# Regrouping the head loads of a one-core attention and gMLP block, taking an early weight load out of the head, and making the instruction order anew

## Chip, cores, metric

The kernel runs on one core of one Trainium2 chip. The metric is the device time in microseconds (us). All times compared below come from runs that were classed as fast, unless the text says otherwise. The sets of runs were made on different chips of the same kind, so each time is to be read against the "before" of its own rounds.

## The reference

The input x has 2048 tokens of 512 values, in bf16.

```python
def _A_ref(x, wqkv, wo):            # called on layernorm(x)
    qkv = split_heads(x @ wqkv)     # 32 heads of 16
    q, k, v = qkv[0], qkv[1], qkv[2]
    phi = lambda t: jnp.where(t > 0, t + 1, jnp.exp(t)) + 1e-06
    pq, pk = phi(q), phi(k)
    kv = einsum('bhsd,bhse->bhde', pk, v)
    ...                             # linear attention, then @ wo
h  = x + _A_ref(layernorm(x), A_wqkv, A_wo)
h2 = h + _B_ref(layernorm(h), B_w_in, B_w_sp, B_b_sp, B_w_out)   # gMLP; w_sp mixes tokens
```

## The kernel before

x is worked on in 16 tiles of 128 tokens, called x0 to x15. The head of the program does this for each tile: load, layernorm statistics and aggregate on VectorE, reciprocal standard deviation `rs` (ScalarE or GpSimd), normalised tile `xn` (VectorE for tiles 0 to 5, ScalarE after that), transposed tile `xnT` (TensorE and a ScalarE copy for tiles 0 to 5, a DMA transpose after that), the "K matmuls" of xnT and wk on TensorE, and then exp, minimum and `pk` on ScalarE and VectorE.

Nothing here is ordered at run time. A Python layer records every operation with its data dependencies and then replays a stored order. That order gives each engine its instruction stream. Waits are generated from the dependencies.

```python
    def schedule(self):
        ids = np.frombuffer(zlib.decompress(base64.b85decode(ORDER)), np.uint16).tolist()
        ...
        self.order = {e: [o for o in self.seq if o.eng == e] for e in self.ENGS}
...
    # loads of the head; first_load puts them behind each other on a queue,
    # `behind` makes the queue wait until another load has landed
    x0 = load_x("SP", 0, 1, 2150)
    load_x("ACT", 1, 1, 2250)
    x2 = load_x("SP", 2, 1, 2500)
    load_x("ACT", 3, 1, 2500)
    wk = [first_load(eng, wqkv[:, c:c + 2, D:2 * D], A_wqkv[c * P:(c + 2) * P, D:2 * D], f"wk{c}", 3500)
          for eng, c in (("SP", 0), ("ACT", 2))]
    for n, lat, behind in ((4, 2000, x2), (6, 2200, x2), (8, 1900, wk[0]), (10, 2100, wk[0]), ...):
        load_x("SP", n, 2, lat, behind)
...
    def stats(src, k, n):
        s = st[k][:, n, :]
        dve(lambda v: v.bn_stats(s[:, 0:6], src[:, n, :]), [src[:, n, :]], [s[:, 0:6]], D)
        return dve(lambda v: v.bn_aggr(s[:, 6:8], s[:, 0:6]), [s[:, 0:6]], [s[:, 6:8]], 14)
...
    warmup(34, 103)                               # matmuls on zeros, no result used
...
        # in k_unit(n), for the two tiles n, n + 1:
                op = stats(x, 0, i)
                if i == 0:
                    second = warmup(16, 60, op)   # waits for the aggregate of x0
...
    # spatial weights, 16 blocks of 128 rows; the first EARLY of them go into the head as whole loads
    for i, t in enumerate(order):
        w = NT // 2 if EARLY <= i < NT // 2 else NT
        for j in range(0, NT, w):
            op = dma_t(wsp[:, j:j + w, t * P:(t + 1) * P], B_w_sp[...], f"wsp{t // TPG}", ...)
```

## Time and profile before

| | before |
|---|---|
| median of the first three runs | 234.14 us |
| span of the profiled run | 231.8 us |
| TensorE (PE) busy | 97% |
| first transposes / first K matmul | 6.35 / 7.90 us |
| K matmuls of tiles 6 and 7 begin | 18.58 us |

The profile page of before gives the span, then busy time with its share of the span and the instruction count for each engine. Further down it gives the shares of the chain of work that ended last.

```profile
span 231.8 us, 3231 instructions
...
PE 224.6 (97%) x1180; PEld 112.1 (48%) x1203; DVE 161.6 (70%) x323; ACT 104.3 (45%) x193; POOL 44.2 (19%) x134
...
PE 86%; DMA 6%; ACT 3%; DVE 2%; issue 1%; SPq 0%
```

TensorE bounds the kernel. The parts of the chain that are not PE lie mostly in the head, and the timeline of PE shows where. Its columns are start, duration, engine, line, operation, operands and count, and in brackets the idle time before it and what ended that.

```profile
1.04 5.51 PE L594 MATMUL psum<-warm 128*128 128x128 bf16 x50 [1.04 <-POOL warm L439]
6.35 1.43 PE L570 MATMUL psum<-ident,xn 128*128 128x128 bf16 x16
7.90 3.52 PE L402 MATMUL psum<-wqkv,xnT 128*128 128x512 bf16 x15
...
14.63 2.75 PE L655 MATMUL psum<-pk,xn 128*128 128x512 bf16 x12
18.58 1.90 PE L402 MATMUL psum<-wqkv,xnT 128*128 128x512 bf16 x7 [1.20 <-DMA xnT<-xn]
```

After the first microsecond one idle stretch stands out, 1.20 us before the K matmuls of tiles 6 and 7. They waited for a DMA transpose. The sync queue's timeline shows what that transpose had to stand behind:

```profile
8.86 5.56 SPq L435 DMA_TRANSPOSE wsp<-in_B_w_sp_dram  x1
14.47 6.10 SPq L435 DMA_TRANSPOSE xnT<-xn  x4
```

The early spatial-weight load holds the queue from 8.86 to 14.42 us. The VectorE timeline of before, from its start:

```profile
3.36 0.70 DVE L511 BATCH_NORM_STATS2 st<-x 128x6 f32<-128x512 bf16 x1 [3.36 <-DMA x<-in_A_x_dram]
4.09 0.18 DVE L512 BATCH_NORM_AGGREGATE st<-st 128x2 f32<-128x6 f32 x1
4.19 1.25 DVE L511 BATCH_NORM_STATS2 st<-x 128x6 f32<-128x512 bf16 x2
5.36 0.30 DVE L512 BATCH_NORM_AGGREGATE st<-st 128x2 f32<-128x6 f32 x2
5.58 0.38 DVE L556 TENSOR_SCALAR xn<-x,st,rs 128x512 bf16<-128x512 bf16 x1
```

The statistics of x0 are aggregated 0.73 us after they began, x2 and x3 follow, and xn0 begins at 5.58 us.

### The profile page before, as it was taken

The numbers are of one execution on the slowest core, as the hardware profiler recorded it, in microseconds if no ns is written. First come the engines' busy times: TensorE is split into PE (matmuls) and PEld (weight loads), VectorE is DVE, ScalarE is ACT, GpSimd is POOL, SyncE is SP. The second block draws the span as 40 slices with busy tenths as digits, with TensorE's granted clock in tenths as the row PEclk, the third lists the DMA queues.
The fourth block names the chain that finished last, engine by engine and source line by source line (L and its number), as shares of the span: only waits on it lengthen the run. The fifth ranks groups of instructions, "written<-read, shape, count | busy, mean of one in ns | idle before, by whom it ended". The sixth has DMA issues, their size and how long they took to land.

```text
span 231.8 us, 3231 instructions
## 1 busy us (share of the span) xinstructions
PE 224.6 (97%) x1180; PEld 112.1 (48%) x1203; DVE 161.6 (70%) x323; ACT 104.3 (45%) x193; POOL 44.2 (19%) x134
## 2 busy tenths in 40 slices
PE   8997999999999999999999999999999999999995
PEld 8543444453445443454544444444455555555452
DVE  4998755646987550237489989979795566785485
ACT  5694754399989876679862010101021211123010
POOL 3436300000466608023771000000000000000000
PEclk9999999999999999999999999999999999999999
DMA  5893259947546635968999700000000000020025
GB/s 182 263 214 70 59 138 230 315 147 181 114 89 136 117 71 121 183 126 188 185 228 197 159 3 0 0 0 0 3 0 1 0 3 0 20 72 3 0 80 191
DMA packets 58864, 23.68 MB, mean 102 GB/s; under 512 B 48480, under 2 KB 58720, under 8 KB 58848
## 3 DMA queue, kind: packets, MB, share of 16 engines
q1 hardware_dynamic: 58144, 22.88, 44.7%
q10 hardware_dynamic: 704, 0.59, 0.8%
q8 instruction: 9, 0.15, 0.3%
q14 instruction: 7, 0.06, 0.1%
HBM read 7.47 MB, written 2.10 MB: 41 GB/s over the span
## 4 chain that ended last, share of the span: by engine, by line
PE 86%; DMA 6%; ACT 3%; DVE 2%; issue 1%; SPq 0%
PE psum L402 70%; PE psum L802 6%; PE psum L655 5%; PE psum L805 4%; DMA x<-in_A_x_dram 3%; DMA xnT<-xn 2%; DMA hnT<-hn 1%; DVE st L511 1%; ACT sh L421 1%; ACT xn L421 1%; ACT e L421 0%; ACT xnT L421 0%; PE psum L751 0%; PE psum L676 0%; PE psum L720 0%
## 5 line engine op out<-in xcount | busy, mean ns | idle before, releaser
L421 ACT ACTIVATE psum<-psum 128x256 f32<-128x256 f32 (+1 forms) x33 | 14.3, 445 | 90.8 <-PE psum L402 63.1
L402 PE MATMUL psum<-wsp,z 128*128 128x512 bf16 x204 | 47.5, 379 | 0.2
L402 PEld LDWEIGHTS psum<-wsp,z 128*128 128x128 bf16 x208 | 20.4, 98 | 22.9
L402 PE MATMUL psum<-hnT,win 128*128 128x512 bf16 x108 | 25.6, 379 | 0.2
L421 ACT ACTIVATE e<-psum 128x1024 bf16<-128x1024 f32 (+1 forms) x18 | 16.7, 926 | 15.2 <-PE psum L402 14.3
L402 PE MATMUL psum<-t,s 128*128 128x512 bf16 x94 | 22.1, 379 | 0.1
L421 ACT ACTIVATE z1T<-psum 128x512 bf16<-128x512 f32 x28 | 16.6, 594 | 4.9 <-PE psum L402 4.8
L802 PE MATMUL psum<-win,hnT 128*128 128x512 bf16 x64 | 16.4, 379 | 0.4 <-DMA hnT<-hn 0.4
L402 PE MATMUL psum<-wout,z1T 128*128 128x256 bf16 (+1 forms) x82 | 16.6, 314 | 0.1
L402 PEld LDWEIGHTS psum<-hnT,win 128*128 128x128 bf16 x112 | 10.0, 98 | 13.2 <-ACT z1T L421 3.8
L402 PE MATMUL psum<-wqkv,xnT 128*128 128x512 bf16 x61 | 14.8, 380 | 1.4 <-DMA xnT<-xn 1.2
L421 ACT ACTIVATE z<-psum 128x896 bf16<-128x896 f32 x16 | 14.5, 909 | 2.9 <-PE psum L805 2.8
L402 PE MATMUL psum<-xnT,wqkv 128*128 128x512 bf16 x61 | 15.1, 379 | 0.3 <-issue 0.2
L655 PE MATMUL psum<-pk,xn 128*128 128x512 bf16 x64 | 15.3, 379 | 0.0
L402 PE MATMUL psum<-m,pqT 128*128 128x512 bf16 x62 | 14.7, 379 | 0.3 <-DVE h L776 0.2
L776 DVE SCALAR_TENSOR_TENSOR h<-psum,x 128x512 bf16<-128x512 f32 x16 | 10.8, 688 | 5.2 <-PE psum L402 5.1
L402 PEld LDWEIGHTS psum<-t,s 128*128 128x128 bf16 x96 | 9.4, 98 | 10.3
L582 DVE TENSOR_SCALAR e<-e 128x1024 bf16<-128x1024 bf16 (+1 forms) x18 | 7.1, 397 | 9.1 <-ACT e L421 9.0
L805 PE MATMUL psum<-win,hnT 128*128 128x384 bf16 x64 | 13.0, 326 | 0.0
L924 DVE TENSOR_TENSOR u<-psum,bsp 128x512 bf16<-128x512 f32 x16 | 11.0, 687 | 2.8 <-PE psum L402 2.7
L556 DVE TENSOR_SCALAR z<-z,st,rs 128x896 bf16<-128x896 bf16 x16 | 7.2, 493 | 7.3 <-POOL rs L519 7.3
L511 DVE BATCH_NORM_STATS2 st<-x 128x6 f32<-128x512 bf16 x15 | 9.7, 677 | 3.6 <-DMA x<-in_A_x_dram 3.6
(113 smaller groups left out, 349.3 us busy)
## 6 DMA issues: line engine op xcount, KB each, us to landing
r<-rcp SPq DMA_DIRECT2D x16, 128.0 KB, 2.6
out_dram<-h SPq DMA_DIRECT2D x15, 128.0 KB, 1.8
win<-in_B_w_in_dram SPq DMA_DIRECT2D x2, 896.0 KB, 6.6
x<-in_A_x_dram SPq DMA_DIRECT2D x6, 256.0 KB, 4.5
wqkv<-in_A_wqkv_dram SPq DMA_DIRECT2D x2, 512.0 KB, 5.2
wout<-in_B_w_out_dram SPq DMA_DIRECT2D x1, 896.0 KB, 7.2
wo<-in_A_wo_dram SPq DMA_DIRECT2D x1, 512.0 KB, 8.3
bsp<-in_B_b_sp_dram SPq DMA_DIRECT2D x1, 512.0 KB, 5.1
```

The lines of the kernel that those rows point to most:

```text
L402: inst = pe.matmul(out_ap, lhsT=a, rhs=b, start=start and i == 0, stop=stop and i == len(pairs) - 1, **kw)
L421: return g.add("ACT", lambda ac: ac.activation(out_ap, in_ap, func, **kw), [in_ap, *extra], [out_ap] + ([accum] if accum is not None else []),
L511: dve(lambda v: v.bn_stats(s[:, 0:6], src[:, n, :]), [src[:, n, :]], [s[:, 0:6]], D)
L556: return dve(lambda v: v.tensor_scalar(dst, src, mean, rst, op0=ALU.subtract, op1=ALU.mult), [src, mean, rst], [dst], w + 460, acc=4)
L582: dve(lambda v: v.tensor_scalar(e, e, 1.0, EPS_PHI, op0=ALU.min, op1=ALU.add), [e], [e], w * GW, acc=4)
L655: inst = pe.matmul(bank(CB[c]), lhsT=xn[:, i, c * P:(c + 1) * P], rhs=pk[:, i, :], start=i == 0, stop=i == NT - 1)
L776: dve(lambda v, n=n, b=b, s=s: v.scalar_tensor_tensor(h[:, n, :], bank(b), 1.0, x[:, n, :], op0=ALU.mult, op1=ALU.add, accum_out=s[:, 0:1] ...
L802: pe.matmul(bank(b), lhsT=hnT[:, c, n * P:(n + 1) * P], rhs=win2[:, c, 0:GW], start=c == 0, stop=c == KD - 1)
L805: inst = pe.matmul(bank(b + 1, F2), lhsT=hnT[:, c, n * P:(n + 1) * P], rhs=win2[:, c, GW:FH], start=c == 0, stop=c == KD - 1)
L924: dve(lambda v: v.tensor_tensor(t, bank(b), add, ALU.add), [bank(b), add], [t], GW, ps=True)
```

## The change

Its intent is to issue fewer and larger loads in the head and to free the sync queue from the early spatial-weight load. The stored order was made anew for this, so the streams of all engines differ. The diff, cut (the two ORDER strings are left out, some switches that are off, and a number of the load of wq). The numbers in the thousands are the times to landing, in ns, that the schedule's model assumes:

```diff
-EARLY = 1
+EARLY = 0
-ORDER = "c-jTQ17HvU..."
+ORDER = "c-jrpgMttU..."
-    x0 = load_x("SP", 0, 1, 2150)
-    load_x("ACT", 1, 1, 2250)
-    x2 = load_x("SP", 2, 1, 2500)
-    load_x("ACT", 3, 1, 2500)
-    wk = [first_load(eng, wqkv[:, c:c + 2, D:2 * D], A_wqkv[c * P:(c + 2) * P, D:2 * D], f"wk{c}", 3500)
-          for eng, c in (("SP", 0), ("ACT", 2))]
-    for n, lat, behind in ((4, 2000, x2), (6, 2200, x2), (8, 1900, wk[0]), ...
+    load_x("SP", 0, 1, 2250)
+    load_x("ACT", 1, 1, 2350)
+    x2 = load_x("SP", 2, 2, 3250)
+    wk = first_load("ACT", wqkv[:, :, D:2 * D], A_wqkv[:, D:2 * D], "wk", 3900)
+    for n, lat, behind in ((4, 1500, x2), (6, 1700, x2), (8, 2000, wk), ...
```

What the new order does to the start of VectorE's stream can be read from the built programs without running them:

```
before: stats x0 | aggr x0 | stats x2, x3 | aggr x2, x3 | xn0 | xn2, xn3 | xn1 | stats x4, x5 ...
after:  stats x0 | stats x4 | aggr x0, x4 | stats x2, x3 | xn0 | aggr x2, x3 | xn1 | stats x5 | xn2, xn3 ...
```

More of the change, by code (lines that the diff above doesn't have):

```diff
@@ L13 @@
 GRAN = 16
-EARLY = 1
+EARLY = 0
 SEM_NS = 45.0
-ORDER = "c-jTQ17HvU00h8Cwq47%ZQHhO+qGrewr$(CZ5wwH5gAbt9Wf9Su@D<^5Eu2800D@ED2Rr5$b~$}jl4*LqyUHz2nE3iiC_qhWJrz_NQp#9j8w>n{3w9JNQ(-ngvO|hifD@XNQl%(gMui6bjW~0NROh(gp4SL;;4eE$c!dvhAgOttSEtOsEO>Tj&A6I?kI_#D23)|fpBPrmgt4v=!-tcfm*16wy2FdXpPdSi+UJ`GAN7sXn-*oi}6^7B{+=bSc-PYiE=294rqh+XoyA_fPol{e&~-u=!i}@g3dUILzsYxn1sn#foYh6Ay|pf2#+ubi&cn#)i{b{IDz9BieU)ENCaUNMq>@uVLGOw3%X(^W?%v4<1|iU78YVH*5eGG;uKz@fg0)sp5qy2V-AL61U6tJ7GW`VU^_NpGqzwZ=3x)^VkdTCH_qWK_F+E`U@Nxa3a;WjF5n_A;U+HQ8gAh_Zr~N(;5FXjHtypN?&2OEA~+u)1Vi#2BJdF+G7{h8F`nQjKHvvF;uk*QAHLu-zTqprBPPMH49!ps!&o$9Gb*DoGNUja<1-H9G91J6H)1dqQ!@`UGdlA!3-hx8(=aX5F+DRdBQvoaOS2ZqeEfr~EJ*P$$}kwSF*|cGCkwGWb1{GkSeQjvl*L$=3Au#z*pj)~gSA<lCE13Fn3xr~m}Oa?OIe4l*qXiBmVH=}l~|co*p6$smJQgDjaZfK*^@Qcm`&J=eVLTWS%RgQgvq#t$(4dlnUc-9hbgp-TbWvEG@MgdjoUbaBiWA~*pZ#sp99#L138Gxxt%+>f-5<d={22=)L1pSjx(4+d%2HY*p1EDg4LN)sgzl1704hC<zRMaR}SM4Hc=L(Q$~$qCQai^o?%vHQ+DN0PUTiE<y9W#S3VU`K^0aZ713E9VR02z2^CXml~fs(S1Fa%9UkQ|-sKg(;Z>H?6TW2y&EkF@;6bkE25#hNj^S92<4*44A&%#4&f#3H;yg~^ah~9OF63cO;wEn9J>KU7KIBQB;yb?Q2cF}3Uf@OU=4r0xHD2c>HdQk<R|~aND^2DCPUIq1RAp7tA3o(X{$&+a)fawcHHBAeB~u%<RXep;2X#~@bygR3RRn!waD`A!g;Xtl<a6HOO+MlazT_>w;wS!NL|x`<J|+}NRAhbU5B}sY-e!CyP!xqyXh~rdRbgcXD4~8ckrFG3s;h>gD~3KZreZ0!!YP`PDvshRnBr-G`e?9ftFC6Kj%I3zhN_+hs;_2ixVmYIrfQJ7tG{|^l~!w-rYle*HCMybQzO(*qclz%G+MnBr16@ddFrkC8lzd7sC8PPC0eMpO5(Aaqyw6xrCOuOTBh~dsLfiWE!wJs+NPvltP@(U?b@Xk+N71*p}jh+L)xvK+Nb?GqCGmQ<4Wk0I;GP(qeMQY#LnfjI;RvquM4`QD@y5$itl8;rcb)A54x<Yx}&?grJK5^+`g{|O6>#=@JBt;L#6U#J<|(4(Nm@MXT8=drE_{e*B8CiS7q=!z125;*AFFk7XQ*uW%O_T6a7bjmEXZ^!*XbcabAaX2#0lehjSWda#m+{HWzR~M{q<(avn!@WJh-t7jkw-a|{=DKF4t^$8-+obP*SIF_&>!7k3HQbA88kBR6&vH*hmIbxD_ULr-!GH+OlrbSw9A8~1h}w{}IBb|qK#1o!hq_jP{{a67kkdk^#=5AiTp@nBbVIoEInS95jObS>9*M|bu{*Ku8UcMnhTR8MmUZ}Mgj^(+r}Cy(?DPxlsg@np|*kViPsvpvsqJl6}n$V)um3%%G&J<g-u)nmQfqrA+kywYpD*6SSG!F@yV+|!}F)$jF2x7E#KyxJ=~-s`==+q~U7ywkh<AMVe{ZU"
@@ new lines @@
+ORDER = "c-jrpgMttU00qE@tj)G<d$VoZwz=81ZQHhO+jiZ}H%vrCMr;Hi5~3g~q9HnBASPlVF3KVv${`1GArTS-AdFxLh2RK>5D>y60+JvpLLwQGBLNa31#%)cQlmWbAP(XqB~l?T@}VFqpaB{o4bmYk@*@!GkpTrz7=@4-4UrLzQ4y6;8JUm;U6B=?(G6Wt4MoueP0<|9&>cO{3!%{pMNkFVkR8=g6)jK$B~TN!&=;dH8pTi?B~c2sF$Q%o7Io1YEzu99Q3h?%2K7)M1F!^3u?UNC5IxZweb66aFb?A}5zDX~6VMJ*FbOL$5NpsL9k3q<FbIb*7{f3WD{vS`a1>!N9IJ2)Couve(Gi_66_YU?(=ZQnF$2djA2TrvYq1(9a0<^+M^Et#k5N}o5QHIEk9Amph1iCz*no}LgxQ#bUD%E7*n=I|iPJcPz1WA%*n-QrgtIt@^SFTPxQHvbfvdQN7kG(Rc#WI5i#xcDTeuJN9)dAA-yj?xAUq@R8{Xm}9^oB6;5**qBR(M-zu+(a;0HeAD}Es~LoozHGCE^0fRP!A5gC?05r)5!f+?Ac8JU++8HJgcig6f|u^Ef0nTBbZj`>)E>6x2kX8!xXOG)Nu9%f-yW@C01U_l155DT+9OH<6jGK|Z3ti|}uz?@vfW~|MwEW#Qr#^x-=1Wd@Xtiy#|%$DrIRjkPtT+KvG%%UvE@~ps$ti;Of#-3clx~#|gY`}&r&P`0J%}l0U+``>V!lZ1(CQQcUoWzu>r}}EjDs087Y|X7~!(I$xcMfAUHfAdI<~B~|9uDVT4q<YoRSJz@IxS@%wq-lEXJ7VX2d36k4rLnkXJ>ZgH16X7uHhhNR3@cYR%K9TWm8UN(G*T+b{%3a<xpPb)?wyT9-U%-on`^e;7o4kNbct-&f;wD;AoEF9FAotcHv+SWI+{DpbD#qZn3CJsHASQm@cunj&L03axLfc3@7j`&v7Tu^8zn&9glJu*Rz2ds*&dLGOzF|ukjeKb2*Q5JR7TtnrZ<jvYE=Ll*+2KUhy^G@DA_t9`Exl-|-QD@iCjLg<7hWTC0uPDv8>uy*j9)I;pd6@I5#11W)n-SMVWMvYg86H~;W2H}W4pv63q2GoSDaD=VzRsiHpcDZ}e4zwrPM@+Q9%qMq?1BPc+U6->cZP1W^-KN(TaSw&S9M{yNJQ58?|l|Ui%f*}=2p%hxtlu*$XLot;|Vf2!bl~}P9Tm95aE7e>5RYSEjNYgb~Gc-iA)J0v@O#?JsBQ#mV6r_QgqNy6Gu^OsznxopPslMv29_pj<nydL*ubCR9dFrXr8l%~ornQ=&#hR$Z-mi69pbeU&RobLATB3zoq@~)d)mo;l+NJ~As4d#5<yxWb+M^xXt9?4GT{^DhKA{9Ysna^8BRZ=yI;Rxgt@k>rLpr8|O5&V8uZy~@RKBLGO6Ci?q$|3uJG!YGx~mVmuY^wIdy4CadZ3hkq^EkW$9kePj^~&9q*sdXw0@=+`m8TX?_5sjH+rkD`lxUEuFU?aANr+y{;j`)^Z1WaJE?8?pXg8y?JN%N5Dw#T4(kjK?+DKA07rI2M|DPLb$(}aCTDj6M|UJgaWv;}UKezr3pti!yNC<BsEav<i@SvDxsFS@w0pRL8@i{<x{({ZiJQ8Y>$;Ddxwredulu{X>${{YxT4E@fLnNwgWSpk-O_E`+HGCNm0a1?JkjMm-c>xolU&s`UEMWY%e6h&?YzO0J;hVK(L+7l9lXiyJ;XCT&C@-@!#u(rJ<D@F+jBhM3%%I$yugdR#3S9=quj}3Jl5U3)Lp&8E4|E{z1nNM*6SR{!5q@J^iHo8)1!S|T|Ca+y~<m>-0Qv7+q~U7ywm>y1b4@<"
@@ L487, in load_x @@
         return first_load(eng, x[:, n:n + w, :], x_d[n * P:(n + w) * P, :], f"x{n}", lat, behind)
-    x0 = load_x("SP", 0, 1, 2150)
-    load_x("ACT", 1, 1, 2250)
-    x2 = load_x("SP", 2, 1, 2500)
-    load_x("ACT", 3, 1, 2500)
-    wk = [first_load(eng, wqkv[:, c:c + 2, D:2 * D], A_wqkv[c * P:(c + 2) * P, D:2 * D], f"wk{c}", 3500)
-          for eng, c in (("SP", 0), ("ACT", 2))]
-    for n, lat, behind in ((4, 2000, x2), (6, 2200, x2), (8, 1900, wk[0]), (10, 2100, wk[0]), (12, 2300, wk[0]),
-                           (14, 2500, wk[0])):
+    load_x("SP", 0, 1, 2250)
+    load_x("ACT", 1, 1, 2350)
+    x2 = load_x("SP", 2, 2, 3250)
+    wk = first_load("ACT", wqkv[:, :, D:2 * D], A_wqkv[:, D:2 * D], "wk", 3900)
+    for n, lat, behind in ((4, 1500, x2), (6, 1700, x2), (8, 2000, wk), (10, 2200, wk), (12, 2400, wk), (14, 2600, wk)):
         load_x("SP", n, 2, lat, behind)
-    first_load("SP", wqkv[:, :, 0:D], A_wqkv[:, 0:D], "wq", 3400)
+    first_load("SP", wqkv[:, :, 0:D], A_wqkv[:, 0:D], "wq", 3500)
     exp_table = g.add("ACT", lambda ac: ac.preload_act_table_set("natural_log_exp_and_others"), [], [], cost=1300)
@@ L611, in bass_sequential_preLN__linear_attn_block__mixer_gmlp__prompt_kernel @@
     HEAD, SINGLE = 6, 4
-    ACTS = (1,)
+    ACTS, ND, LEAD, lead = (1,), (), 0, []
     QSPLIT, KSPLIT, CACT = (6, 7), (), 2
@@ L618, in k_unit @@
         b = next_pair()
+        first = len(g.ops)
         for i in (n, n + 1):
@@ L631, in k_unit @@
                     rstd_act(st[0], rs[0], i, 1, 6)
+        if n == 2 and LEAD:
+            for op in g.ops[first:]:
+                if op.eng == "DVE":
+                    op.soft.add(lead[LEAD - 1].i)
         if n == 2:
@@ L634, in k_unit @@
         elif n:
-            rstd(st[0], rs[0], n, 2, 6, n >= HEAD)
+            rstd(st[0], rs[0], n, 2, 6, n >= HEAD or n in ND or n + 1 in ND)
         for i in (n, n + 1):
-            norm("DVE" if n < HEAD else "ACT", xn[:, i, :], x[:, i, :], st[0], rs[0], i, 6, D)
+            lead.append(norm("DVE" if n < HEAD and i not in ND else "ACT", xn[:, i, :], x[:, i, :], st[0], rs[0], i, 6, D))
             if n < HEAD:
@@ L647, in k_unit @@
             for i in (n, n + 1):
-                phi(pk[:, i:i + 1, :], b + i % 2, 1)
+                phi(pk[:, i:i + 1, :], b + i % 2, 1, i in KSPLIT)
         else:
```

## The prediction

> **What bounds the kernel now.** From about 18.6 us to the end TensorE does. The busy table gives PE 224.6 of 231.8 us, and the chain that ended last is PE for 86% of the span, almost without a gap after 18.58 us. So only the head can win or lose time. There the chain runs: x0 and x2 landed (to 4.00), the load of x4/x5 that was queued behind x2 (4.00 to 7.58), VectorE statistics and xn (to 11.48), ScalarE, then two DMA transposes (14.47 to 18.58). The waits view has one PE wait of note, 1.2 us for xnT at 17.4 us; the timeline of the sync queue shows why: the spatial-weight transpose occupies it from 8.86 to 14.42. VectorE is 99% busy from 10 to 20 us.
>
> **What the change does.**
> 1. Removes that 5.56 us issue. Worth at most the 1.2 us PE wait (0.5%). The same bytes come later as two half loads, well before the spatial matmuls at 118.8 us[...]: about 0.
> 2. x2 and x3 as one 256 KB load on the sync queue, wk as one 512 KB load on the scalar queue: the same 1 MB, two issues fewer (about 0.45 us each). x0, x1 as before (3.4 us). But "x2" now lands only when 256 KB have moved, with wk beside it: about 4.8 us instead of 3.98, estimated from the bytes per slice of before. The loads of x4 and x6 wait for x2, so x4 lands at about 7.7 us (7.2 to 8.5).
> 3. The reordering is the important part. In the new VectorE stream the second statistics instruction is that of x4, ahead of the aggregate of x0. [...] So x0's aggregate, which ran at 4.09 us, waits for x4's landing: about 8.4. Then two more statistics (1.25 us) precede xn0: about 10.0 instead of 5.58. xn2 and xn3 come 4 to 5 us later than before.
>
> **On the critical path.** Stepping through the new orders with durations of the trace (statistics 0.6, xn 0.35, copy 0.5, exp 0.6, pk 0.6, four K matmuls 0.87): first transposes at 10.0 instead of 6.35, first K matmul at 11.3 instead of 7.90, pk0 to pk3 about 4 us later, K matmuls of tiles 6 and 7 at about 21.4 instead of 18.58. The 1.2 us saved is inside this. PE has no later gaps in which to regain the rest: +2.8 us.
>
> PE also has nothing to do from about 4.8 to 8.4 us, since the second warm-up group waits for x0's aggregate. [...] In before the 50 warm-up matmuls took 5.5 us (about 110 ns each), while K matmuls started 0.22 us apart. I allow 0.7 us for cold matmuls.
>
> **Prediction:** 237.6 us (80%: 235.4 to 239.6). Faster by over 2%: 1%; within 2%: 74%; slower by over 2%: 25%.
>
> **Right if** the VectorE timeline shows one statistics instruction at 3.4 us, a gap of about 4 us ended by the load of x, and xn0 near 10 us; PE idle before the second warm-up group; the first K matmul at 11 to 12.5 us; a constant shift of 2.5 to 4.5 us from 25 us on.
>
> **Wrong if** x4 lands near 6.5 us (then +1.5), if matmuls run cold to 16 us or later (+1.5 more), or if wv and wo, now behind other late loads, land after their need at 50 to 55 us (a new wait, up to 2 us). If VectorE did not block on x4, the result would be about 232.8.

## The result

| | before | after |
|---|---|---|
| median, fast runs of the same rounds | 233.76 us (232.53 to 234.48) | 236.41 us (235.51 to 237.18) |
| ratio after / before | | 1.0117, 95% interval 1.008 to 1.0153 |
| first transposes / first K matmul | 6.35 / 7.90 us | 10.19 / 11.51 us |
| K matmuls of tiles 6 and 7 begin | 18.58 us | 22.45 us |

A ratio is the mean time of one kernel's fast runs over that of the other's fast runs of the same rounds, so it is not quite the ratio of the medians. A second set of five rounds of the same kernel is the yardstick for three later experiments.

**after_again.** Edit: none.

> The kernel after, unchanged, timed again in five rounds as the yardstick for the next three: ratio to before 1.009 to 1.014.

Measured: 236.19 us against 233.22, ratio 1.0131 (1.0104 to 1.0159). The change makes the kernel about 3 us slower, within the 2% band but clear of noise.

From here on the kernel after has line numbers of its own: L508 and L509 are its statistics and aggregate, L553 its xn, L591 its warm-up, L567 its transposes. Its page:

```profile
span 235.2 us, 3244 instructions
...
PE 227.0 (97%) x1203; PEld 113.0 (48%) x1203; DVE 161.3 (69%) x323; ACT 104.0 (44%) x193; POOL 44.2 (19%) x134
...
PE 90%; DMA 4%; DVE 2%; ACT 1%; SPq 1%; issue 0%
```

The busy shares are those of before, so they do not tell what happened. The VectorE timeline does:

```profile
3.55 0.69 DVE L508 BATCH_NORM_STATS2 st<-x 128x6 f32<-128x512 bf16 x1 [3.55 <-DMA x<-in_A_x_dram]
7.68 0.69 DVE L508 BATCH_NORM_STATS2 st<-x 128x6 f32<-128x512 bf16 x1 [3.43 <-DMA x<-in_A_x_dram]
8.29 0.30 DVE L509 BATCH_NORM_AGGREGATE st<-st 128x2 f32<-128x6 f32 x2
8.50 1.25 DVE L508 BATCH_NORM_STATS2 st<-x 128x6 f32<-128x512 bf16 x2
9.67 0.40 DVE L553 TENSOR_SCALAR xn<-x,st,rs 128x512 bf16<-128x512 bf16 x1
```

The second line is the statistics of x4. VectorE stood idle for 3.43 us until x4 landed. The data for the next useful instruction, the aggregate of x0, had been there since about 4.2 us. xn0 begins at 9.67 instead of 5.58 us. The PE timeline of after:

```profile
1.04 3.54 PE L591 MATMUL psum<-warm 128*128 128x128 bf16 x34 [1.04 <-POOL warm L439]
8.51 1.89 PE L591 MATMUL psum<-warm 128*128 128x128 bf16 x16 [3.92 <-DVE st L509]
10.19 1.06 PE L567 MATMUL psum<-ident,xn 128*128 128x128 bf16 x8
11.51 1.89 PE L402 MATMUL psum<-wqkv,xnT 128*128 128x512 bf16 x4 [0.26 <-ACT xnT L421]
13.19 1.06 PE L567 MATMUL psum<-ident,xn 128*128 128x128 bf16 x8
...
22.45 1.89 PE L402 MATMUL psum<-wqkv,xnT 128*128 128x512 bf16 x8
```

PE was idle for 3.92 us ahead of the second warm-up group. The first four K matmuls took from 11.51 to 13.19 us, 0.42 us each, where before needed 0.22. The granted clock explains that. The next view gives, for PE, the busy time in each stretch, its clock, and the DMA share and rate:

```profile
6.00:8.00 2.00, 0.00 (x0) 0.89 0.86 271
8.00:10.00 2.00, 1.49 (x15) 0.50 0.96 299
10.00:12.00 2.00, 1.74 (x14) 0.50 1.03 345
12.00:14.00 2.00, 2.00 (x12) 0.50 0.37 131
14.00:16.00 2.00, 2.00 (x12) 0.90 0.00 0
```

The clock was at half rate from about 7.6 to 14.4 us: a mean of 0.89 over 2 us means 2 x (1 - 0.89) / 0.5 = 0.44 us at half rate before 8.00, and likewise 0.4 us after 14.00. Tiles 6 and 7 begin 3.87 us later than before. After 22 us nothing adds to this. A little is given back: before had waits of 0.3 us (for ScalarE's m) and 0.4 us (for a DMA transpose of hn) between 55 and 66 us which after does not have, and the first spatial matmul block stands at 123.67 us against 120.32, 3.35 us later. The spans differ by 3.4 us.

These are the traces of the costlier kind of run of after. Of its 12 timed runs in the two sets, the four with a mean clock of 0.985 or 0.986 took 236.88 to 237.50 us, and the other eight 235.50 to 236.56 us. Both profiled runs are among the four. So the 3.4 us of the traces lie above the 2.65 and 2.97 us of the medians.

Why would an order put the statistics of x4 second? The kernel's own file suggests an answer. The time model in its `schedule` was replayed. In after the model starts the load of x4 at 1.00 us and has its data at 3.00 us, counted from the first load, which the trace has at 0.79 us. The trace has 4.85 and 7.65 us. The load of x4 must wait until x2 has landed. But in after x2 is also the load just ahead of it on its queue, and the model counts no landing time for an operation that is listed as such a neighbour. In before the half wk stood between them, and the model started x4 at 3.54 us. That the new order was made with this model is likely, but not shown.

### The profile page after: what moved, and what is told of

Read it like the earlier page. It is cut to its first block, busy times and chain, and to the rows that moved or that the text cites. A ratio compares the mean times of both kernels' runs of the same rounds, so it can differ in the third digit from the quotient of the medians.

```text
span 235.2 us, 3244 instructions
## 1 busy us (share of the span) xinstructions
PE 227.0 (97%) x1203; PEld 113.0 (48%) x1203; DVE 161.3 (69%) x323; ACT 104.0 (44%) x193; POOL 44.2 (19%) x134
## 4 chain that ended last, share of the span: by engine, by line
PE 90%; DMA 4%; DVE 2%; ACT 1%; SPq 1%; issue 0%
PE psum L402 72%; PE psum L657 6%; PE psum L804 6%; PE psum L807 4%; DMA x<-in_A_x_dram 3%; DMA r<-rcp 1%; PE psum L591 1%; SPq L744 1%; PE psum L567 1%; DVE h L778 1%; DVE pqT L766 1%; ACT pqT L421 0%; PE psum L678 0%; PE psum L687 0%; PE psum L753 0%; ACT r L421 0%
## 5 line engine op out<-in xcount | busy, mean ns | idle before, releaser
L402 PE MATMUL psum<-hnT,win 128*128 128x512 bf16 x112 | 26.1, 379 | 0.0
L402 PE MATMUL psum<-wqkv,xnT 128*128 128x512 bf16 x64 | 16.2, 397 | 0.3 <-ACT xnT L421 0.3
L508 DVE BATCH_NORM_STATS2 st<-x 128x6 f32<-128x512 bf16 x15 | 10.0, 678 | 7.0 <-DMA x<-in_A_x_dram 7.0
L553 DVE TENSOR_SCALAR hn<-h,st,rs 128x512 bf16<-128x512 bf16 x16 | 6.2, 406 | 11.3 <-POOL rs L544 11.0
L820 DVE BATCH_NORM_STATS2 st<-z 128x6 f32<-128x512 bf16 x9 | 6.1, 690 | 9.7 <-ACT z L421 9.7
```

Source lines behind the costliest of these rows:

```text
L402: inst = pe.matmul(out_ap, lhsT=a, rhs=b, start=start and i == 0, stop=stop and i == len(pairs) - 1, **kw)
L553: return dve(lambda v: v.tensor_scalar(dst, src, mean, rst, op0=ALU.subtract, op1=ALU.mult), [src, mean, rst], [dst], w + 460, acc=4)
L820: dve(lambda v, n=n, s=s: v.bn_stats(s[:, 0:6], z2[:, n, 0:GW]), [z2[:, n, 0:GW]], [s[:, 0:6]], GW)
```

## The experiments

Two theories stood against each other. The *order theory* says that the loss is VectorE's wait for x4 ahead of the aggregate of x0. The *load theory* says that the loss comes from x2, x3 and wk landing later. A third question is how much of the loss is the cold clock, that is, matmuls at half rate (the first four K matmuls of after took 0.42 us each, where before needed 0.22). All times are medians, and "before" is that of the same rounds. The programs were built again: each differs from its parent in the instructions named and in no others (in experiment 6 only a wait changes). Every run is recorded as correct.

To move instructions, the recorded operations were given names, and their places in the stored list were exchanged just before it is replayed. Waits are generated anew from the dependencies.

### 1. After, with the statistics of x4 and x5 moved back

```diff
         ids = ... ORDER ...
+        for a, b in [("stats4", "aggr5"), ("aggr4", "aggr5"), ("stats5", "aggr5")]:
+            a, b = self.named[a].i, self.named[b].i
+            ids.remove(a)
+            ids.insert(ids.index(b), a)      # a now stands just before b
```

> The kernel after, with three VectorE instructions (statistics of x4, its aggregate, statistics of x5) moved behind xn3; loads and all other streams as after. Order theory (the loss is VectorE's in-order wait for x4 ahead of x0's aggregate): the 3.4 us wait moves behind xn3 and shrinks to below 1 us, first transposes at 6.3 to 6.7 us, first K matmul at 7.7 to 8.3 us at full rate, time about 232.8 us, ratio to before 0.990 to 1.000. Load theory (the loss is that x2 with x3 and the whole wk land later): first K matmul still late, ratio stays 1.008 or more.

Measured: 233.48 us against 233.17, ratio 1.0023 (0.9997 to 1.0049). The PE timeline:

```profile
6.57 0.40 PE L573 MATMUL psum<-ident,xn 128*128 128x128 bf16 x4 [1.05 <-DVE xn L559]
7.45 0.40 PE L573 MATMUL psum<-ident,xn 128*128 128x128 bf16 x4 [0.48 <-DVE xn L559]
7.90 0.81 PE L407 MATMUL psum<-wqkv,xnT 128*128 128x512 bf16 x3
...
12.55 0.40 PE L573 MATMUL psum<-ident,xn 128*128 128x128 bf16 x4 [0.76 <-DVE pk L590]
```

Line numbers are again the experiment's own. Three VectorE instructions in another place take back 2.66 us of the 2.97 us that after loses (0.31 against 2.97 us above before, in different rounds; 2.34 of 2.65 us by the first set). The load theory expected no gain at all, and it falls. The ratio missed the upper end of what I had expected by 0.2%. There is a second wait, 0.76 us for VectorE's pk0 at 12.55 us: pk0 ran at 11.81 us here, and at 10.44 us in before. Both orders have the statistics of x4 to x7 ahead of pk0. Here they begin 0.80 us later (8.38 against 7.58 us), and xn4 stands ahead of pk0 too.

### 2. Before, with one instruction moved forward

```diff
+        for a, b in [("stats4", "aggr0")]:   # in before.py, placed as above
```

> The kernel before, with one VectorE instruction (statistics of x4) moved ahead of the aggregate of x0; loads and all other streams as before. Order theory: x4 lands at about 7.6 us, xn0 at 9 to 10 us, first K matmul near 11.3 us and at half rate, ratio to before 1.009 to 1.015. Load theory: the loads are those of before, so ratio 0.998 to 1.003.

Measured: 236.79 us against 233.17, ratio 1.0159 (1.0133 to 1.0185). Its VectorE timeline repeats the picture of after, with the loads of before:

```profile
3.50 0.69 DVE L516 BATCH_NORM_STATS2 st<-x 128x6 f32<-128x512 bf16 x1 [3.50 <-DMA x<-in_A_x_dram]
7.34 0.69 DVE L516 BATCH_NORM_STATS2 st<-x 128x6 f32<-128x512 bf16 x1 [3.15 <-DMA x<-in_A_x_dram]
7.96 0.17 DVE L517 BATCH_NORM_AGGREGATE st<-st 128x2 f32<-128x6 f32 x1
```

One instruction of 0.69 us, early by nine places, costs 3.6 us of the whole kernel. Within the noise this is what the whole change costs (1.0131, 1.0104 to 1.0159). Two expectations were missed: the ratio lies just above its range, and the first K matmul came at 12.26 us instead of 11.3. From there to 16.12 us the 16 K matmuls were 0.24 us apart, so most of them were not at half rate.

### 3. Before, with the new loads alone

```diff
 # in before.py: the new load_x and wk lines of the change; EARLY stays 1; the stored order
 # loses the entries of the loads that are gone (x3, one half of wk), all else in place
```

> The kernel before with the new head loads alone (x2 and x3 as one, wk whole on the scalar queue); the early spatial-weight load stays and every engine's order is that of before. Order theory: x2 lands at about 4.8 us, xn0 0.5 us later than before, which the wait for xnT at 17.4 us mostly hides: ratio 0.998 to 1.003. Load theory: 1.008 or more.

Measured: 233.53 us against 233.17, ratio 1.0017 (0.9987 to 1.0046). x2 landed at 4.80 us and xn0 began at 6.22 instead of 5.58 us. This hardly reaches the end. The load theory's 1.008 is outside the interval.

### 4. Before, without the early spatial-weight load

```diff
-EARLY = 1
+EARLY = 0
+    order.insert(7, order.pop(0))     # block 0 goes behind the other half loads, as two halves
```

> The kernel before with the early spatial-weight load taken from the head (its two halves come after the other half loads); nothing else moves. If the 1.2 us PE wait for xnT is due to that 5.56 us issue, it disappears and the ratio is 0.994 to 0.998. If the xnT transposes are bound by something else (ScalarE's xn, or the queue itself), the wait stays and the ratio is 0.999 to 1.002.

Measured: 232.17 us against 233.17, ratio 0.9957 (0.994 to 0.9975). The PE line of tiles 6 and 7, which had a wait of 1.20 us before it at 18.58 us in before, now reads:

```profile
17.23 1.89 PE L406 MATMUL psum<-wqkv,xnT 128*128 128x512 bf16 x7
```

The wait is gone, and the measured 1.00 us is most of it. This half of the change's intent was right.

### 5 and 8. After, with a longer warm-up that does not wait for x0

```diff
-                    second = warmup(16, 60, op)
+                    second = warmup(66, 60)      # experiment 5; 100 in experiment 8
```

> The kernel after, but the second warm-up group no longer waits for x0's aggregate and has 66 matmuls instead of 16, so TensorE has no long idle stretch before the first transposes; all other streams as after. If cold matmuls are a real part of the loss, the first K matmuls start 0.22 us apart instead of 0.42, and the time falls 0.5 to 1.0 us below that of after (ratio to before 1.007 to 1.010). If the clock is irrelevant because VectorE paces the head, it stays within 0.3 us of after.

Measured in 5: 236.6 us against 233.22, ratio 1.0148 (1.0104 to 1.0192), which neither expectation allows. The runs came in two kinds: 235.27, 235.37 and 235.72 us at a mean granted clock of 1.0, and 237.49, 237.70 and 238.23 us at 0.993. Another look at the same kernel caught the second kind:

> The same kernel as in the fifth experiment, one profile more, in the hope of a run of the slower kind: then the profile shows granted clock 0.993 and a stretch of K matmuls 0.42 us apart after the warm-up. If it is of the faster kind (clock 1.0, about 235.5 us) it tells nothing new.

Measured: 237.4 us at 0.993 (a single run, so its state is unknown). PE's timeline and then its stretches show what happened:

```profile
1.04 7.55 PE L591 MATMUL psum<-warm 128*128 128x128 bf16 x100 [1.04 <-POOL warm L439]
10.07 0.85 PE L567 MATMUL psum<-ident,xn 128*128 128x128 bf16 x8 [1.48 <-DVE xn L553]
11.15 1.43 PE L402 MATMUL psum<-wqkv,xnT 128*128 128x512 bf16 x4 [0.23 <-ACT xnT L421]
```

```profile
10.00:12.00 2.00, 1.64 (x12) 0.92 0.77 264
12.00:14.00 2.00, 2.00 (x12) 0.50 0.65 227
14.00:16.00 2.00, 2.00 (x8) 0.73 0.01 2
16.00:18.00 2.00, 2.00 (x14) 1.00 0.00 0
```

The 100 warm-up matmuls took 7.55 us here (8.58 us in the first kind), so the warm-up was over at 8.59 us, PE waited 1.48 us for xn0, and the clock fell to half for 3.4 us (0.32 + 2 + 1.08, worked out from the three clocks), just as the real matmuls began. In the first kind of run (profiled in experiment 5) the warm-up lasted to 9.63 us, and no such stretch followed. There the K matmuls of tiles 6 and 7 begin 1.76 us earlier than in the second kind, which has them at 22.36 us:

```profile
20.60 1.89 PE L402 MATMUL psum<-wqkv,xnT 128*128 128x512 bf16 x8
```

> As the kernel after with the ungated second warm-up group, but 100 matmuls in it instead of 66, so that TensorE is busy right up to the first transposes. The 66 gave two kinds of run: 235.3 to 235.7 us at a granted clock of 1.0 and 237.5 to 238.2 us at 0.993, which I take to be one stretch of half rate after the warm-up ran out. If so, the slower kind disappears and all runs are at 235.2 to 236.2 us, ratio 1.007 to 1.012, and the cold clock is worth 0.5 to 1 us of the loss. If the two kinds remain, the idle stretch is not what makes them.

Measured in 8: 235.86 us against 233.19, ratio 1.0103 (1.0081 to 1.0125), all six runs between 235.23 and 236.35 us. The slow kind did not occur. In its profiled run PE's waits view lists no wait between the warm-up and the first transposes, where the second look at experiment 5 has 1.48 us. This fits an idle PE between warm-up and work as the cause.

How much of the loss is the cold clock? By total times, 0.3 us from the medians of 8 and after_again (236.19 - 235.86, different rounds, intervals overlap), though in 8 the warm-up itself held back the first transposes: they came at 10.67 us, and at 9.94 us in 5. The fast kind of 5 gives 0.8 us (236.19 - 235.37), but those runs were picked afterwards. The traces give more: from the first transposes to the K matmuls of tiles 6 and 7, after takes 12.26 us and experiments 5 and 8 take 10.66 and 10.65 us. That is 1.6 us, in the costlier kind of run of after. So the cold clock is worth 0.3 to 0.8 us in the medians and up to 1.6 us in a single run.

### 6. After, with x4 and x6 loaded without waiting for x2

```diff
-    for n, lat, behind in ((4, 1500, x2), (6, 1700, x2), ...
+    for n, lat, behind in ((4, 1500, None), (6, 1700, None), ...
```

> The kernel after, but the loads of x4 and x6 no longer wait for x2 to land; same queue order, same VectorE order. Order theory: the time follows the landing of x4: it lands at 5.5 to 6.2 us instead of 7.7, xn0 comes as much earlier, and 1.2 to 2 us of the loss are gone (ratio to before 1.003 to 1.007), although x2 and wk land no earlier. Load theory (what counts is when x2 and wk land): no gain, ratio 1.010 or more.

Measured: 236.28 us against 233.22, ratio 1.0121 (1.0092 to 1.0151). That is no measurable gain over after (1.0131), so the expectation failed; read by the ranges set before the run, the result is on the side of the load theory. VectorE's lines say that half of it did happen:

```profile
6.80 0.69 DVE L508 BATCH_NORM_STATS2 st<-x 128x6 f32<-128x512 bf16 x1 [2.49 <-DMA x<-in_A_x_dram]
7.41 0.30 DVE L509 BATCH_NORM_AGGREGATE st<-st 128x2 f32<-128x6 f32 x2
...
8.80 0.40 DVE L553 TENSOR_SCALAR xn<-x,st,rs 128x512 bf16<-128x512 bf16 x1
```

x4 landed at 6.80 us, only 0.88 us earlier than in after. xn0 came 0.87 us earlier. In the profiled runs the first spatial matmuls stood at 123.06 us, against 123.84 in after_again. So 0.8 us was saved in that pair of runs, but those two had different clock histories (a mean of 1.0 against 0.985), and the timed runs do not show it. The dose was too small for the spread of the runs (after alone took 235.5 to 237.5 us, at mean clocks of 1.0 to 0.985). The experiment is inconclusive on the load theory; experiments 1 to 3 decide that.

### 7. Both parts of the change, without the new order

```diff
 # before.py with the edits of experiments 3 and 4 together; compute engines keep the order of before
```

> The kernel before with both parts of the change's intent (the new head loads, and no early spatial-weight load) but with the order of before on every compute engine. If the two parts add up: 1.0017 times 0.9957, so 0.995 to 1.000, about 1 us faster at best; if removing the early load is worth nothing beside the later x2, 1.000 to 1.003. Either way the re-made order would be the whole of the loss.

Measured: 232.10 us against 233.22, ratio 0.995 (0.9932 to 0.9968). Its PE line of tiles 6 and 7:

```profile
17.52 1.89 PE L411 MATMUL psum<-wqkv,xnT 128*128 128x512 bf16 x8
```

This beats both kernels: 1.1 us below before, and 4.1 us below after in the same rounds (236.19 - 232.10). The intended change is worth 0.5%. By experiments 3 and 4, the early weight load gives all that could be measured of it. The re-made order takes that and 3 us more.

### 9. After, with VectorE's head order mended further

```diff
+        # besides the moves of experiment 1:
+        ("stats6","min1"), ("xn4","min1"), ("xn5","min1"), ("stats7","stats9"),
+        ("aggr6","stats9"), ("aggr7","stats9"), ("pk1","stats7")
 # cut: the list is then sorted by dependencies; every other engine keeps its order
```

> The kernel after with VectorE's head order mended further than in the first experiment: besides statistics of x4 and x5 behind xn3, the statistics and aggregates of x6 to x9 go behind what TensorE waits for (pk0, xn4, xn5, pk1). Other engines as after. If the order on VectorE is the whole loss, K matmuls of tiles 6 and 7 start at about 17.5 us as in the version that kept the old order (18.75 in the first experiment), and the ratio is 0.993 to 0.999. If something in the other engines' new order costs as well, it stays at 1.000 to 1.004.

Measured: ratio 1.0131 (1.0102 to 1.0161), five fast runs of 235.1 to 237.16 us. The profiled run had a granted clock of 0.755 and took 299.25 us; it is not used. The expectation failed.

> The same kernel as in the ninth experiment, one profile more, since its first fell into a run at a granted clock of 0.755. It came out slower than the first experiment, against the expectation. If ScalarE is the reason (its in-order stream has xn of tile 6 ahead of the copy of xnT of tile 4, and I made the statistics of x6 and x7 late), ScalarE shows an idle stretch of 1 us or more before xn of tile 6, ended by GpSimd's rs, at about 13 to 15 us, and TensorE waits for xnT behind it. If not, ScalarE is busy there.

Measured: 236.91 us (a single run, state unknown). ScalarE's timeline, then PE's:

```profile
11.10 0.60 ACT L433 ACTIVATE e<-psum 128x512 bf16<-128x512 f32 x1 [0.21 <-PE psum L414]
15.45 0.81 ACT L433 ACTIVATE xn<-x,rs 128x512 bf16<-128x512 bf16 x1 [3.75 <-POOL rs L534]
16.17 0.58 ACT L433 ACTIVATE xnT<-psum 128x512 bf16<-128x512 bf16 x1
```

```profile
14.10 0.39 PE L580 MATMUL psum<-ident,xn 128*128 128x128 bf16 x4
16.80 3.23 PE L414 MATMUL psum<-wqkv,xnT 128*128 128x512 bf16 x8 [2.32 <-ACT xnT L433]
```

My mending made the very mistake I was studying. By moving the aggregates of x6 and x7 back on VectorE, I made xn6 late. On ScalarE xn6 stands ahead of the copy of xnT4, which TensorE needed. ScalarE idled for 3.75 us, most of it with the transposes of tile 4 done (11.97 to 12.37 us), PE idled for 2.32 us, and the clock dropped (to 0.50 from 18 to 20 us; the K matmuls at 16.80 took 0.4 us each). What the remaining 1.4 us between experiments 1 and 7 is made of (0.31 above before against 1.12 below) is therefore not settled. The traces place most of it: at tiles 6 and 7 experiment 1 is 1.23 us behind experiment 7 (18.75 against 17.52 us), although its first K matmul was 0.36 us ahead (7.90 against 8.26 us). The wait for pk0 lies in between. Here that wait was gone and the transposes of tile 5 came at 14.10 us instead of 15.06, before ScalarE lost more than that. So the attempt did not test the total cleanly.

## Why the prediction was right

- **The mechanism.** The prediction named one instruction, the statistics of x4 ahead of the aggregate of x0, as the cause of the loss. That VectorE would stand still there was my assumption when I predicted. The trace of after shows it: a 3.43 us idle stretch with the aggregate's input ready. Experiments 1 and 2 show it from both sides: moving three instructions back takes 2.66 us off, and moving one forward adds 3.6 us. It is not the whole cost of the order: without the block the prediction expected 232.8 us, 1.3 below its before, and experiment 1 came out 0.31 above. The 1.4 us between experiments 1 and 7 were not in its sum.
- **The steps in time.** x4 at about 7.7 us: measured 7.68. xn0 at about 10.0: measured 9.67. First transposes at 10.0: 10.19. First K matmul at 11.3: 11.51. x2 at about 4.8: 4.85 in the chain.
- **The size.** Predicted 237.6 against a before of 234.14, so +3.5 us. Measured +2.65 us by the medians of the first set and +2.97 by the second.
- **The early load.** "Worth at most the 1.2 us": experiment 4 gives 1.00 us with the old order. What it is worth with the new order was not tested.
- **The loads.** The regrouping was held to be almost nothing in itself: experiment 3 gives +0.36 us, an interval that includes zero.
- **The cold clock.** Predicted 0.7 us, an estimate of mine; 0.3 to 0.8 in the medians, 1.6 in the head of the profiled run. In the trace of after PE is idle from 4.59 us for 3.92 us, and the clock is 0.50 from about 7.6 us, 3.0 us into the idle stretch, to 14.4 us.
- **Where it was off.** Tiles 6 and 7 came 3.87 us late in the profiled run, where 2.8 plus 0.7 for the cold clock was forecast. The split was further off than the sum: in experiment 5, with the K matmuls at full rate, they came at 20.60 us, only 2.0 us late (x4 landed 0.2 us earlier there). The delay was estimated too large and the clock too small, and the two partly cancel; that part of the agreement is luck. "PE has no later gaps in which to regain the rest" is not quite so either: 0.5 us was given back by 124 us, where before had waited for things that after has ready. The feared late landing of wv and wo did not happen: the waits view of PE after 20 us holds only one 0.2 us wait.

## What to carry to other kernels

When a scheduler re-makes an order for new load times, read the first ten instructions of each engine's stream and ask of each: what if its load is late? Here VectorE stood idle for 3.43 us in after, and ScalarE for 3.75 us in the second look at experiment 9, at an instruction whose data came late, with the data of the next useful one there for all or most of that time. Such an instruction must not stand ahead, unless its landing time is measured and not assumed. Keep the order when you test a change of loads: here the two load edits together gained 1.1 us, nearly all of it from the early weight load, and the new order cost 4.1 us. And mending one engine's stream alone can create the same blockage on the next engine: in the second look at experiment 9, ScalarE's idle stretch left PE idle for 2.32 us.

## What the traces show of the clock

- In three traces the granted clock fell after idle stretches of PE of different lengths. In after it was at 0.50 from about 7.6 us, 3.0 us into an idle stretch of PE. In the second look at experiment 5 PE was idle for 1.48 us and for 0.23 us, with 8 transposes between. Apart from these no matmul ran for 2.56 us (8.59 to 11.15), and the clock was at 0.50 for 3.4 us from about 11.7 us. In experiment 9 an idle stretch of 2.32 us preceded a half rate that began at about 17.2 us and also lasted 3.4 us.
- The granted clock of a record read 1.0 over matmuls that were as slow as at a recorded 0.50. In experiment 6 the record reads 1.0 from 10 to 12 us, while the first four 128x512 K matmuls took 1.68 us (10.64 to 12.32), 0.42 us each; in after, at a recorded 0.50, they took the same 1.68 us. Why the record and the times of experiment 6 disagree is not shown.
- The mean clock of a run came in steps of about 0.007 (1.0, 0.993, 0.985). Each step fits one stretch of 3.4 us at half rate in 235 us (3.4 x 0.5 / 235 = 0.0072): the second look at experiment 5, at 0.993, has one of 3.4 us, and after, at 0.985, is at 0.50 for about 6.8 us (7.6 to 14.4).
